# RWKV-5 attention into a multiplicative FFN: the FFN's first products start inside token chunk 0, on weight strips of 256 columns, and one predicated copy serves both heads of a pair

## The chip, the cores and the metric

The kernel runs on one core of one Trainium2 chip. The metric is the device time of one execution in microseconds (us); lower is better. The notes on the profile use its names for the engines: PE is TensorE (matrix products), PEld its weight loads, DVE is VectorE, ACT is ScalarE, POOL is GpSimd and SP is SyncE, which issues the transfers.

## The reference

```python
def attention(r, k, v, w, u):                 # (4, 8, 768, 48) = batch, heads, tokens, head size; float32
    state = zeros(B, H, D, D)
    for t in range(S):
        cur = einsum('bhd,bhe->bhde', u * k[:, :, t], v[:, :, t])
        y[:, :, t] = einsum('bhd,bhde->bhe', r[:, :, t], state + cur)
        state = w[:, :, None] * state + einsum('bhd,bhe->bhde', k[:, :, t], v[:, :, t])

x = y.transpose(0, 2, 1, 3).reshape(3072, 384)
out = (((x @ w1) * (x @ w2)) @ w3) @ w_out    # w1, w2: 384 x 1024; w3: 1024 x 1024; w_out: 1024 x 384
```

The four FFN weights come as float64; the attention's inputs are float32 and the result is float32.

## The kernel before

**Units.** The 768 tokens of each of the four sequences are cut into six chunks of 128. A unit is one chunk of one sequence, for all eight heads, and the units run chunk by chunk: unit n is chunk n // 4 of sequence n % 4. Heads are handled in four pairs, so that two heads of 48, padded to 64, fill 128 partitions.

**What a unit does.** `load` fetches k, r and v. `scale(n)` multiplies k and r by powers of the decay on VectorE (L277, tile `krs`), forms the sums for the diagonal on VectorE (L282 to L284, tiles `ruk` and `dg`) and writes them as diagonal matrices on ScalarE (L289, tile `AT`). `turn(n)` transposes k and r on TensorE and copies them out on ScalarE (`kT`, `rT`). `pairs(n)` computes the 128 x 128 products of keys and receptances of each head on TensorE (L307) and copies the causal half over the diagonal matrices with two predicated copies on VectorE (L310). `output(n)` adds the contribution of the state (L355, from chunk 1 on) and of the chunk itself (L363), and ScalarE copies the result, transposed, into `xT[c]`. `update(n)` computes k times v (L381) and adds it to the state `st` (L388, or L390 and L393).

**The FFN.** It works on whole token chunks of 4 x 128 = 512 tokens. `ab(c, j)` computes 128 of the 1024 hidden columns of x w1 (L403) and of x w2 (L408), ScalarE copies the first out (L405) and VectorE multiplies the two into a tile `abt` (L409). w3 and w_out are multiplied into one matrix `w34` once: `fold(j)` transposes 128 rows of w3 (L263) and multiplies them with w_out (L267). `o(c, b)` multiplies the `abt` tiles by `w34` (L414) and stores 128 rows of the result.

**The weights.** A float64 piece lands in one of three tiles `raw` as 64-bit words. `convert` rebuilds float32 from the two 32-bit halves in seven steps: |x| on ScalarE (L231), then on VectorE a product (L232), a mask with a shift (L234), a mask with an or (L235), a mask (L237), the low half scaled (L238) and the last add (L239). w1 and w2 are taken in twelve pieces of 128 rows by 512 columns: first the six that hold columns 0 to 511, then the other six.

**The order.** `beside[c]` is a list of FFN steps for each chunk. Beside each unit's steps (scale and turn of unit n+1; then pairs of n+1, output and update of n) an eighth of its chunk's list is put. In chunk 0 that is only the first six weight pieces; chunk 1 has the other six and `ab(0, j)` for all j; chunk 2 `ab(1, j)`, w_out and the folds 0 to 2; chunk 3 the other folds, `o(0, b)` and `ab(2, j)`:

```python
beside = [
    W12[0],
    merge(W12[1], AB(0, range(KH))) + AB(0, range(KH, KF)),
    merge(AB(1), WO + W3(range(3))),
    merge(AB(2, range(KH)), W3(range(3, KF))) + O(0) + AB(2, range(KH, KF)),
```

A planner then turns the written order into a queue for each engine, from its own costs and from what each instruction needs; each engine works through its queue in that order. The functions that the change touches:

Of the kernel before, what the change touches and what calls it, by code (L numbers as in the profile page):

```python
# [8 lines left out]
F32 = mybir.dt.float32  # L9
I32 = mybir.dt.int32  # L10
U32 = mybir.dt.uint32
U64 = mybir.dt.uint64
# [4 lines left out]
PSUM = bass.MemoryType.PSUM  # L17
# [3 lines left out]
def kernel(  # L21
# [27 lines left out]
    nc = tc.nc  # L49
    B, H, S, D = r.shape  # L50
    P = 128
    C = 128
# [3 lines left out]
    NP = H // 2  # L56
    DM = H * D
    DF = moe_w3.shape[0]
    KM = DM // P
    KF = DF // P  # L60
    NT = B * C
    LEVELS = 7
    PIECE = 512
    W_LOW, W_HIGH = 0.6, 1.6
    Q = 32
    PD = 2 * D
# [3 lines left out]
    def rows(i):  # L70
        return slice(i * PAD, (i + 1) * PAD)
# [11 lines left out]
    krin = [const.tile([C, 2, H, D], F32, name=f"krin{i}") for i in range(NIN)]  # L83
    vnat = [const.tile([C, H, PAD], F32, name=f"vnat{i}") for i in range(NV)]
    krs = [const.tile([C, 2, H, PAD], F32, name=f"krs{i}") for i in range(NS)]
    raws = [const.tile([P, PIECE], U64, name=f"raw{i}") for i in range(NRAW)]
    st = [const.tile([P, NP, PD], F32, name=f"st{b}") for b in range(B)]
    wucol = const.tile([P, NP, 1], F32)
    nc.vector.memset(wucol, 1.0)
# [10 lines left out]
    NU = len(units)  # L100

    def load(n):
        if n >= NU:
# [9 lines left out]
    w34 = const.tile([P, KF, DM], F32)  # L113


    ab_pieces = [(dst[:, q, js], src[q * P:(q + 1) * P, js])
                 for js in (slice(z * PIECE, (z + 1) * PIECE) for z in range(DF // PIECE))
                 for q in range(KM) for dst, src in ((w1, moe_w1), (w2, moe_w2))]
    sent = [0]

    def fetch(piece):

        dst, src = piece
        if src.dtype != U64:
            nc.sync.dma_start(out=dst, in_=src)
            return None
        raw = raws[sent[0] % NRAW][:, :src.shape[1]]
        sent[0] += 1
        nc.sync.dma_start(out=raw, in_=src)
        return raw  # L130
# [57 lines left out]
    def body(arm, fast):  # L188
        tab = arm.enter_context(tc.tile_pool(name="tab", bufs=1))
        work = arm.enter_context(tc.tile_pool(name="work", bufs=2))  # L190
        psT = arm.enter_context(tc.tile_pool(name="psT", bufs=2, space=PSUM))
        psA = arm.enter_context(tc.tile_pool(name="psA", bufs=2, space=PSUM))
        psM = arm.enter_context(tc.tile_pool(name="psM", bufs=2, space=PSUM))
        psF = arm.enter_context(tc.tile_pool(name="psF", bufs=2, space=PSUM))

# [26 lines left out]
        def convert(piece, raw):  # L222
            dst, src = piece
            if src.dtype != U64:
                return
            n = src.shape[1]
            lo, hi = (raw.bitcast(U32).rearrange("p (n z) -> p n z", z=2)[:, :, z] for z in range(2))
            t, power = (work.tile([P, PIECE], F32, tag="cv", bufs=4, name=nm)[:, :n] for nm in ("t", "power"))
            tb, hb, pb = t.bitcast(U32), dst.bitcast(U32), power.bitcast(U32)

            nc.scalar.activation(out=power, in_=hi.bitcast(F32), func=ABS)  # L231
            nc.vector.scalar_tensor_tensor(dst, power, 1.125 * 2.0 ** -15, hi.bitcast(F32), ALU.is_ge, ALU.mult)  # L232

            nc.vector.tensor_scalar(tb, hb, 0x07FFFFFF, 3, ALU.bitwise_and, ALU.logical_shift_left)  # L234
            nc.vector.scalar_tensor_tensor(hb, hb, 0xC0000000, tb, ALU.bitwise_and, ALU.bitwise_or)  # L235

            nc.vector.tensor_scalar(pb, hb, 0xFF800000, None, ALU.bitwise_and)  # L237
            nc.vector.scalar_tensor_tensor(t, lo, 2.0 ** -52, power, ALU.mult, ALU.mult)  # L238
            nc.vector.tensor_add(dst, dst, t)  # L239

        def weight(piece):
            convert(piece, fetch(piece))
# [3 lines left out]

        def out_weight(c):
            wo[c] = work.tile([P, DM], F32, tag="wo", bufs=KF, name=f"wo{c}")
            weight((wo[c], moe_w_out[c * P:(c + 1) * P, :]))

        def w3_weight(j, z):
            if z == 0:
                w3n[j] = work.tile([P, DF], F32, tag="w3", bufs=3, name=f"w3n{j}")
            js = slice(z * PIECE, (z + 1) * PIECE)
            weight((w3n[j][:, js], moe_w3[j * P:(j + 1) * P, js]))

        def fold(j):
            w3T = work.tile([P, KF, P], F32, tag="w3", bufs=3, name=f"w3T{j}")
# [14 lines left out]
        def scale(n):  # L273

            kr = krin[n % NIN]
            if fast:
                nc.vector.tensor_mul(krs[n % NS][:, :, :, :D], kr, pn[:, :, :, :D])  # L277
            else:
                nc.scalar.copy(out=krs[n % NS][:, :, :, :D], in_=kr)
            ruk = work.tile([C, H, D], F32, tag="ruk", bufs=2, name=f"ruk{n}")  # L280
            dg = work.tile([C, H], F32, tag="dg", bufs=2, name=f"dg{n}")
            nc.vector.tensor_mul(ruk, kr[:, 0], kr[:, 1])  # L282
            nc.vector.tensor_mul(ruk, ruk, ub)
            nc.vector.tensor_reduce(dg, ruk, AX.X, ALU.add)  # L284
            AT[n] = work.tile([C, 2, NP, C], F32, tag="AT", bufs=2, name=f"AT{n}")
            for p in range(NP):
                for i in range(2):
                    h = 2 * p + i
                    nc.scalar.activation(out=AT[n][:, i, p, :], in_=ident, func=COPY, scale=dg[:, h:h + 1])  # L289
# [10 lines left out]
        def pairs(n):  # L300

            if fast:

                ps = [psA.tile([C, NP, C], F32, tag="a", name=f"ps_a{n}_{i}") for i in range(2)]
                for p in range(NP):
                    for i in range(2):
                        nc.tensor.matmul(ps[i][:, p, :], lhsT=kT[n][rows(i), p, :], rhs=rT[n][rows(i), p, :],  # L307
                                         start=True, stop=True)
                for i in range(2):
                    nc.vector.copy_predicated(AT[n][:, i], later.bitcast(I32)[:, None, :].to_broadcast([C, NP, C]), ps[i])  # L310
                return
            for l in range(LEVELS):
                L = 1 << l
# [81 lines left out]

        abt = {}

        def ab(c, j):
            abt[c, j] = work.tile([P, NT], F32, tag="abt", bufs=2 * KF + KF // 2, name=f"abt{c}_{j}")
            js = slice(j * P, (j + 1) * P)  # L400
            pa = psF.tile([P, NT], F32, tag="f", name=f"ps_a{c}_{j}")
            for q in range(KM):
                nc.tensor.matmul(pa, lhsT=w1[:, q, js], rhs=xT[c][:, q, :], start=(q == 0), stop=(q == KM - 1))  # L403
            a = work.tile([P, NT], F32, tag="sa", bufs=2, name=f"a{c}_{j}")
            nc.scalar.copy(out=a, in_=pa)  # L405
            pb = psF.tile([P, NT], F32, tag="f", name=f"ps_b{c}_{j}")
            for q in range(KM):
                nc.tensor.matmul(pb, lhsT=w2[:, q, js], rhs=xT[c][:, q, :], start=(q == 0), stop=(q == KM - 1))  # L408
            nc.vector.tensor_mul(abt[c, j], pb, a)  # L409

        def o(c, b):
            po = psF.tile([P, DM], F32, tag="f", name=f"ps_o{c}_{b}")
# [6 lines left out]
            nc.sync.dma_start(out=out[row:row + C, :], in_=osb)  # L419


        def AB(c, js=range(KF)):
            return [lambda c=c, j=j: ab(c, j) for j in js]

        def O(c):
            return [lambda c=c, b=b: o(c, b) for b in range(B)]

        def first(i):
            if i not in landed:
                landed[i] = fetch(ab_pieces[i])  # L430
            convert(ab_pieces[i], landed[i])

        half = len(ab_pieces) // 2
        W12 = [[lambda i=i: first(i) for i in range(z * half, (z + 1) * half)] for z in range(2)]
        WO = [lambda c=c: out_weight(c) for c in range(KF)]

        def W3(js):
            return [s for j in js for s in ([lambda j=j, z=z: w3_weight(j, z) for z in range(DF // PIECE)]
                                            + [lambda j=j: fold(j)])]

        def merge(*lists):

            keyed = [((i + 0.5) / len(x), m, s) for m, x in enumerate(lists) for i, s in enumerate(x)]
            return [s for _, _, s in sorted(keyed, key=lambda e: e[:2])]

        KH = KF // 2
        beside = [
            W12[0],
            merge(W12[1], AB(0, range(KH))) + AB(0, range(KH, KF)),
            merge(AB(1), WO + W3(range(3))),  # L450
            merge(AB(2, range(KH)), W3(range(3, KF))) + O(0) + AB(2, range(KH, KF)),
            merge(O(1) + O(2), AB(3)),
            merge(O(3), AB(4)),
        ]
# [4 lines left out]
        turn(0)  # L459
        pairs(0)  # L460
        for c in range(NCH):
            done = 0
            for b in range(B):
                n = c * B + b
                load(n + 2)
                steps = []
                if n + 1 < NU:
                    steps += [lambda: (scale(n + 1), turn(n + 1))]
                steps += [lambda: (n + 1 < NU and pairs(n + 1), output(n), update(n))]
                for i, step in enumerate(steps):  # L470
                    step()
                    due = len(beside[c]) * (b * len(steps) + i + 1) // (B * len(steps))
                    while done < due:
                        beside[c][done]()
                        done += 1
        for step in tail:
            step()
        landed.clear()
# [38 lines left out]
```

## Time and profile before

| | |
|---|---|
| median of 3 runs | 564.75 us (563.84 to 565.81) |
| the profiled execution: its time | 564.53 us |
| its span in the profile | 562.7 us |
| PE busy, share of the span | 539.0 us, 96% |
| PE weight loads busy | 307.2 us, 55% |
| VectorE busy | 255.5 us, 45% |
| ScalarE busy | 169.2 us, 30% |
| TensorE's mean granted clock | 0.989 |
| DMA | 37.52 MB, mean 67 GB/s |

Shares are over the whole span, but the kernel has stages with different limits, so the slices in time say more than the means. A busy TensorE is not one at its peak: matmuls are pipelined, and one of 128x512 lasts 597 ns in the table while the next begins 430 ns after it. The matmul records count passes: an fp32 matmul shows as two.

### The profile page before, as it was taken

The numbers are of one execution on the slowest core, as the hardware profiler recorded it, in microseconds if no ns is written. First come the engines' busy times: TensorE is split into PE (matmuls) and PEld (weight loads), VectorE is DVE, ScalarE is ACT, GpSimd is POOL, SyncE is SP. The second block draws the span as 40 slices with busy tenths as digits, with TensorE's granted clock in tenths as the row PEclk, the third lists the DMA queues.
The fourth block names the chain that finished last, engine by engine and source line by source line (L and its number), as shares of the span: only waits on it lengthen the run. The fifth ranks groups of instructions, "written<-read, shape, count | busy, mean of one in ns | idle before, by whom it ended". The sixth has DMA issues, their size and how long they took to land.

```text
span 562.7 us, 8088 instructions
## 1 busy us (share of the span) xinstructions
PE 539.0 (96%) x3304; PEld 307.2 (55%) x3304; DVE 255.5 (45%) x495; ACT 169.2 (30%) x400; POOL 3.6 (1%) x17
## 2 busy tenths in 40 slices
PE   3869999999999999999999999999999999999996
PEld 2656555455655565565645556555555555544453
DVE  5999999998674696840220414233211100001100
ACT  3745544454433263331211213122132110111010
POOL 2000000000000000000000000000000000000000
PEclk9969999999999999999999999999999999999999
DMA  7956543554233243220110202021010000000001
GB/s 161 227 134 160 153 112 90 149 170 132 43 115 77 76 120 97 57 43 21 50 29 14 57 14 57 15 57 30 16 29 14 1 15 14 29 28 0 0 16 47
DMA packets 84129, 37.52 MB, mean 67 GB/s; under 512 B 76273, under 2 KB 79474, under 8 KB 84082
## 3 DMA queue, kind: packets, MB, share of 16 engines
q1 hardware_dynamic: 84082, 36.91, 25.0%
q8 instruction: 28, 0.46, 0.3%
q14 instruction: 19, 0.16, 0.1%
HBM read 32.18 MB, written 4.72 MB: 66 GB/s over the span
## 4 chain that ended last, share of the span: by engine, by line
PE 90%; DVE 6%; DMA 1%; issue 1%; ACT 1%; SPq 0%; DVEq 0%; ACTq 0%
PE ps_o L414 22%; PE ps_b L408 22%; PE ps_a L403 22%; PE ps_w L267 7%; PE ps_a L307 5%; PE ps_y L363 4%; PE ps_y L355 3%; PE ps_kT L295 2%; PE ps_s L381 2%; PE ps_rT L295 2%; PE ps_w3T L263 1%; DVE t L238 1%; DVE AT L310 1%; DMA raw<-in_moe_w_dram 1%; DVE w L239 1%
## 5 line engine op out<-in xcount | busy, mean ns | idle before, releaser
L403 PE MATMUL ps_a<-xT,w 128*128 128x512 f32 x288 | 133.4, 597 | 0.7 <-DVE w L239 0.7
L409 DVE TENSOR_TENSOR abt<-ps_b,a 128x512 f32<-128x512 f32 x48 | 33.1, 691 | 221.8 <-PE ps_b L408 196.5
L408 PE MATMUL ps_b<-xT,w 128*128 128x512 f32 x288 | 132.5, 594 | 0.1
L414 PE MATMUL ps_o<-w,abt 128*128 128x384 f32 x384 | 127.2, 488 | 0.0
L414 PEld LDWEIGHTS ps_o<-w,abt 128*128 128x128 f32 x384 | 72.0, 190 | 49.2 <-issue 2.0
L408 PEld LDWEIGHTS ps_b<-xT,w 128*128 128x128 f32 x288 | 54.2, 190 | 67.1 <-issue 63.5
L403 PEld LDWEIGHTS ps_a<-xT,w 128*128 128x128 f32 x288 | 52.9, 190 | 56.8 <-issue 50.1
L289 ACT ACTIVATE AT<-ident,dg 128x128 f32<-128x128 f32 x192 | 59.1, 391 | 1.7 <-DVE dg L284 1.7
L405 ACT COPY a<-ps_a 128x512 f32<-128x512 f32 x48 | 28.0, 584 | 104.3 <-PE ps_a L403 104.3
L310 DVE COPY_PREDICATED AT<-later,ps_a 128x512 f32<-128x512 int32 x48 | 33.0, 730 | 31.2 <-PE ps_a L307 30.9
L417 ACT COPY osb<-ps_o 128x384 f32<-128x384 f32 x24 | 11.5, 479 | 108.7 <-PE ps_o L414 85.7
L267 PE MATMUL ps_w<-wo,w3T 128*128 128x384 f32 x128 | 43.1, 490 | 0.0
L307 PEld LDWEIGHTS ps_a<-rT,kT 64*128 64x128 f32 x384 | 25.9, 198 | 19.2 <-issue 11.3
L307 PE MATMUL ps_a<-rT,kT 64*128 64x128 f32 x384 | 31.7, 299 | 2.7 <-ACT rT L298 2.7
L367 ACT COPY xT<-ps_y 128x384 f32<-128x384 f32 x24 | 11.5, 478 | 74.3 <-PE ps_y L363 74.3
L231 ACT ACTIVATE power<-raw 128x512 f32<-128x512 f32 (+1 forms) x36 | 23.6, 655 | 31.5 <-DVE t L238 19.7
L267 PEld LDWEIGHTS ps_w<-wo,w3T 128*128 128x128 f32 x128 | 23.7, 190 | 15.7 <-ACT w3T L264 0.6
L363 PE MATMUL ps_y<-AT,vnat 128*32 128x128 f32 x768 | 29.1, 274 | 2.4 <-DVE AT L310 1.3
L298 ACT COPY kT<-ps_kT 128x512 f32<-128x512 f32 x24 | 14.0, 585 | 40.7 <-PE ps_kT L295 40.7
L363 PEld LDWEIGHTS ps_y<-AT,vnat 128*32 128x32 f32 x768 | 22.4, 110 | 5.2 <-DVE AT L310 2.5
L277 DVE TENSOR_TENSOR krs<-krin,pn_in 128x768 f32<-128x768 f32 x24 | 22.9, 956 | 3.8 <-ACT pn_in L179 2.8
L238 DVE SCALAR_TENSOR_TENSOR t<-raw,power 128x512 f32<-128x512 uint32 (+1 forms) x36 | 23.6, 655 | 0.2
(64 smaller groups left out, 339.1 us busy)
## 6 DMA issues: line engine op xcount, KB each, us to landing
raw<-in_moe_w_dram SPq DMA_DIRECT2D x28, 512.0 KB, 3.6
krin<-in_k_dram SPq DMA_DIRECT2D x24, 192.0 KB, 2.8
krin<-in_r_dram SPq DMA_DIRECT2D x24, 192.0 KB, 3.4
vnat<-in_v_dram SPq DMA_DIRECT2D x24, 192.0 KB, 2.8
out_dram<-osb SPq DMA_DIRECT2D x24, 192.0 KB, 1.9
raw<-in_moe_w_out_dram SPq DMA_DIRECT2D x8, 384.0 KB, 2.9
ub<-in_u_dram SPq DMA_DIRECT2D x1, 192.0 KB, 5.3
wucol<-in_w_dram SPq DMA_DIRECT2D x2, 0.8 KB, 1.9
```

What stands on the lines that cost most here:

```text
L231: nc.scalar.activation(out=power, in_=hi.bitcast(F32), func=ABS)
L238: nc.vector.scalar_tensor_tensor(t, lo, 2.0 ** -52, power, ALU.mult, ALU.mult)
L267: nc.tensor.matmul(ps, lhsT=w3T[:, kc, :], rhs=wo[kc], start=(kc == 0), stop=(kc == KF - 1))
L289: nc.scalar.activation(out=AT[n][:, i, p, :], in_=ident, func=COPY, scale=dg[:, h:h + 1])
L307: nc.tensor.matmul(ps[i][:, p, :], lhsT=kT[n][rows(i), p, :], rhs=rT[n][rows(i), p, :], start=True, stop=True)
L310: nc.vector.copy_predicated(AT[n][:, i], later.bitcast(I32)[:, None, :].to_broadcast([C, NP, C]), ps[i])
L363: nc.tensor.matmul(to(q, g), lhsT=vv[:, p, x:x + Q], rhs=AT[n][:, i, p, :], start=(not c and m < P // Q), stop=True, skip_group_check=True)
L403: nc.tensor.matmul(pa, lhsT=w1[:, q, js], rhs=xT[c][:, q, :], start=(q == 0), stop=(q == KM - 1))
L405: nc.scalar.copy(out=a, in_=pa)
L408: nc.tensor.matmul(pb, lhsT=w2[:, q, js], rhs=xT[c][:, q, :], start=(q == 0), stop=(q == KM - 1))
L409: nc.vector.tensor_mul(abt[c, j], pb, a)
L414: nc.tensor.matmul(po, lhsT=abt[c, j][:, b * C:(b + 1) * C], rhs=w34[:, j, :], start=(j == 0), stop=(j == KF - 1))
```

## The change

The weights w1 and w2 come in eight strips of 256 columns by all 384 rows (three groups of 128), w1 and w2 in turn, instead of twelve pieces of 128 rows by 512 columns. The tiles `raw` and the scratch of `convert` grow from 512 to 768 elements a partition, and the scratch has three buffers instead of four.

In chunk 0, after unit 1's output, `ab(0, 0)` and `ab(0, 1)` are computed for the first 256 tokens, that is the two sequences that are ready; for the other 256 at the end of the chunk, and behind them `ab(0, 2)` and `ab(0, 3)`. Chunk 1 keeps `ab(0, 4)` to `ab(0, 7)`. The lists of chunks 0 and 1 say for each of eight places what stands there; the lists of later chunks are cut in eighths as before.

`pairs` writes the products of both heads of the pairs into one PSUM tile of two banks, in one buffer, and one predicated copy of 1024 elements a partition takes the place of two of 512.

`abt` has 18 buffers instead of 20 and `ruk` one instead of two, and in chunk 3 two of `ab(2, j)` instead of four are merged with the folds.

```diff
+    STRIP = 256
+    RAW = KM * STRIP
...
-    ab_pieces = [(dst[:, q, js], src[q * P:(q + 1) * P, js])
-                 for js in (slice(z * PIECE, (z + 1) * PIECE) for z in range(DF // PIECE))
-                 for q in range(KM) for dst, src in ((w1, moe_w1), (w2, moe_w2))]
+    ab_pieces = [(dst[:, :, js], src.rearrange("(q p) n -> p q n", p=P)[:, :, js])
+                 for js in (slice(z * STRIP, (z + 1) * STRIP) for z in range(DF // STRIP))
+                 for dst, src in ((w1, moe_w1), (w2, moe_w2))]
...
-        psA = arm.enter_context(tc.tile_pool(name="psA", bufs=2, space=PSUM))
+        psA = arm.enter_context(tc.tile_pool(name="psA", bufs=1 if fast else 2, space=PSUM))
...
-            n = src.shape[1]
-            lo, hi = (raw.bitcast(U32).rearrange("p (n z) -> p n z", z=2)[:, :, z] for z in range(2))
-            t, power = (work.tile([P, PIECE], F32, tag="cv", bufs=4, name=nm)[:, :n] for nm in ("t", "power"))
+            _, m, n = src.shape
+            lo, hi = (raw.bitcast(U32).rearrange("p m (n z) -> p m n z", z=2)[:, :, :, z] for z in range(2))
+            t, power = (work.tile([P, RAW], F32, tag="cv", bufs=3, name=nm)[:, :m * n].rearrange("p (m n) -> p m n", m=m)
+                        for nm in ("t", "power"))
...
-                ps = [psA.tile([C, NP, C], F32, tag="a", name=f"ps_a{n}_{i}") for i in range(2)]
+                ps = psA.tile([C, 2, NP, C], F32, tag="a", name=f"ps_a{n}")
...
-                for i in range(2):
-                    nc.vector.copy_predicated(AT[n][:, i], later.bitcast(I32)[:, None, :].to_broadcast([C, NP, C]), ps[i])
+                nc.vector.copy_predicated(AT[n].rearrange("s i p t -> s (i p) t"),
+                                          later.bitcast(I32)[:, None, :].to_broadcast([C, H, C]),
+                                          ps.rearrange("s i p t -> s (i p) t"))
...
-        def ab(c, j):
-            abt[c, j] = work.tile([P, NT], F32, tag="abt", bufs=2 * KF + KF // 2, name=f"abt{c}_{j}")
+        def ab(c, j, ts=slice(0, NT)):
+            if (c, j) not in abt:
+                abt[c, j] = work.tile([P, NT], F32, tag="abt", bufs=2 * KF + 2, name=f"abt{c}_{j}")
...
-                nc.tensor.matmul(pa, lhsT=w1[:, q, js], rhs=xT[c][:, q, :], start=(q == 0), stop=(q == KM - 1))
+                nc.tensor.matmul(pa[:, :n], lhsT=w1[:, q, js], rhs=xT[c][:, q, ts], start=(q == 0), stop=(q == KM - 1))
...
-            nc.vector.tensor_mul(abt[c, j], pb, a)
+            nc.vector.tensor_mul(abt[c, j][:, ts], pb[:, :n], a[:, :n])
...
-        half = len(ab_pieces) // 2
-        W12 = [[lambda i=i: first(i) for i in range(z * half, (z + 1) * half)] for z in range(2)]
+        W12 = [[lambda i=i: first(i) for i in (2 * z, 2 * z + 1)] for z in range(DF // STRIP)]
...
+        halves = [slice(0, NT // 2), slice(NT // 2, NT)]
+        none = []
         beside = [
-            W12[0],
-            merge(W12[1], AB(0, range(KH))) + AB(0, range(KH, KF)),
+            [none, none, none, W12[0] + AB(0, range(0, 2), halves[0]), none, W12[1][:1], none,
+             AB(0, range(0, 2), halves[1]) + W12[1][1:] + AB(0, range(2, 4))],
+            [none, W12[2], none, AB(0, range(4, 6)), none, W12[3], none, AB(0, range(6, 8))],
             merge(AB(1), WO + W3(range(3))),
-            merge(AB(2, range(KH)), W3(range(3, KF))) + O(0) + AB(2, range(KH, KF)),
+            merge(AB(2, range(2)), W3(range(3, KF))) + O(0) + AB(2, range(2, KF)),
```

## The prediction

> **What bounds the kernel now.** I read the slices of the span first, then stage windows, then the order of time at the last place where TensorE waits, then the groups of VectorE with their shapes kept apart.
>
> ```profile
> PE   3869999999999999999999999999999999999996
> DVE  5999999998674696840220414233211100001100
> PEclk9969999999999999999999999999999999999999
> ...
> 28.00:42.00 14.00, 8.85 (x90) 7.17 (x90) 13.19 (x26) 6.96 (x18) 0.00 (x0) 0.63 0.54 136
> 42.00:56.00 14.00, 13.61 (x189) 8.53 (x191) 13.55 (x27) 7.90 (x22) 0.00 (x0) 1.00 0.66 159
> 84.00:98.00 14.00, 13.32 (x99) 7.10 (x94) 13.66 (x28) 6.07 (x15) 0.00 (x0) 1.00 0.31 85
> 98.00:112.00 14.00, 14.00 (x63) 7.00 (x55) 13.91 (x33) 6.79 (x16) 0.00 (x0) 1.00 0.58 155
> 112.00:126.00 14.00, 14.00 (x120) 7.96 (x119) 13.96 (x31) 6.75 (x17) 0.00 (x0) 1.00 0.56 154
> ```
>
> After a window's length come the busy times of PE, weight loads, VectorE, ScalarE, GpSimd, the granted clock, DMA share and GB/s. VectorE is busy from 14 to 126 us almost without a hole; TensorE has holes only early. The last that matters is this one:
>
> ```profile
> 84.13 0.68 DVE L239 TENSOR_TENSOR w<-w,t 128x512 f32<-128x512 f32 x1
> ...
> 84.86 1.13 PE L403 MATMUL ps_a<-xT,w 128*128 128x512 f32 x2 [0.68 <-DVE w L239]
> ...
> 109.27 0.60 PE L295 MATMUL ps_kT<-ident,krs 128*128 128x128 f32 x4
> ```
>
> At 84.86 the matmul that had waited for the last add (L239) of a w1 piece starts. From there TensorE runs on without a hole that counts (one of 0.24 us near 206) until its last matmul near 558; the chain of waits gives it 90% of the span. At 109.27 the last `ab` of token chunk 0, `ab(0, 7)`, is through and unit 8's transposes begin. Behind this point both kernels have the same matmuls. **So the change is worth the shift of this landmark, and what TensorE waits afterwards.** What sets it is VectorE: six of the seven steps by which a weight piece is rebuilt from float64 stand on it, between the attention's own steps.
>
> ```profile
> L310 DVE COPY_PREDICATED AT<-later,ps_a 128x512 f32<-128x512 int32 x8 | 5.8, 726 | 0.1
> L235 DVE SCALAR_TENSOR_TENSOR w<-w,t 128x512 uint32<-128x512 uint32 x8 | 5.5, 686 | 0.1
> ...
> L277 DVE TENSOR_TENSOR krs<-krin,pn_in 128x768 f32<-128x768 f32 x4 | 3.8, 950 | 0.0
> L234 DVE TENSOR_SCALAR t<-w 128x512 uint32<-128x512 uint32 x8 | 3.3, 416 | 0.0
> L237 DVE TENSOR_SCALAR power<-w 128x512 uint32<-128x512 uint32 x8 | 3.3, 414 | 0.0
> ```
>
> The two mask steps L234 and L237 take 415 ns where L235 takes 686 for as many elements[...]. Durations overlap, so I count from start to start: 0.60 us for a two-source step of 512, 0.47 for one of 384, 0.87 for one of 768 (L277, 62.12 to 62.99); a mask step 0.335 for 512, 0.27 for 384; a predicated copy 0.62.
>
> [...] In the trace both are one run of 512, and the steps are fast; no run shows another shape yet. [...] at 20.63 VectorE waits 0.42 us for the state update's matmuls (L381) and the next weight step comes after. [...] The trace has 0.50 from 31.5 to 38.5 after a window with 1.85 of 3.5 us busy[...].
>
> **The change, part by part.** The VectorE orders of the two built programs can be laid side by side. In the new one, the scaling of unit 8's keys stands behind all eight strips and eight predicated copies. TensorE behind it: turn, ScalarE's copy of rT, pairs, update of unit 7, two of three matmuls of `ps_a`, then `ps_b`, `ps_a`, `ps_b`, which end at the landmark. From turn to pairs 1.8 us (76.36 to 78.18), pairs 1.1 (115.38 to 116.48), the rest of y and the update 0.7, four passes of 0.43 and three times 2.58 (from the starts between 98.86 and 109.27) 9.45, the handoff 0.1: 13.15 us.
>
> *Strips.* Twelve pieces of 512 columns become eight of 3 x 256 = 768 elements. A piece cost 4 x 0.60 + 2 x 0.335 = 3.07, twelve 36.8 us. A strip costs 4 x 0.87 plus two mask steps. Those now read `w1[:, :, js]`, three rows of 256 that do not touch, and write a tile that is one run of 768: outermost 3 against 768, [...] 0.87 as for L277; [...] they would be 0.47 (0.067 per 128 elements from 384 to 512, on top of 0.335). No row of before shows it: between 0.47 and 0.87 I take 0.87, **16 x 0.40 = 6.4 us** apart[...]. Eight strips: 8 x 5.22 = 41.8 us, 5.0 more than before; at the fast rate 35.4.
>
> *One predicated copy.* 1024 elements for twice 512: 0.62 + 0.53 (four times the 0.13 from 384 to 512 elements) = 1.15 against 1.24, so 0.09 a unit, 0.7 us over the eight at the landmark; bounds 0 and 0.7[...]. The single PSUM buffer of two banks holds what two of one bank held: the next unit's pairs wait for this unit's copy in both.
>
> *Halves.* `ab(0, 0)` and `ab(0, 1)` become four of 256 tokens: 24 matmul passes of about 0.215 for 12 of 0.43, nothing on TensorE as weight loads (0.19) still fit under them; two more ScalarE copies, beside other work; two more VectorE products, 4 x 0.335 for 2 x 0.60, 0.14 us.
>
> *Sum on VectorE* from its start at 10.65 to unit 8's scaling: 9 scalings 7.8, 32 steps of 384 for ruk and dg 15.0, 8 copies 9.2, 7 state updates 5.3 and two decays 0.9, strips 41.8, six products 3.7, three steps of the first w_out piece 1.2: 84.9, so 95.5. To this come waits. The same sum for before ends at 80.95 where the trace has 84.81: 3.9 us, of which 2.7 are named waits. For after: the two first strips are 768 KB instead of 512 and stand in the queue before units 1 and 2's loads, so unit 1's scaling starts 262 KB/(227 GB/s of the page's second slice) = 1.2 us later, 1.8 in all; 0.3 where the last update matmul of unit 1 is queued behind unit 2's turn; 1.1 of small gaps as before; 0.4 for half-clock matmuls between 35 and 42. I take 3.6, bounds 2 and 6. Later queue steps cost nothing here: raw tile 4 is asked for near 33 and used at 52, tile 6 near 52 and 66. Landmark: 95.5 + 3.6 + 13.15 = **112.25, 3.0 us later than 109.27**.
>
> *Fewer buffers for abt (18), conversion scratch (3) and ruk (1).* The plan for chunk 3 now puts fold 3 right behind fold 2 and fold 5 right behind fold 4, with no `ab` between. Each waits for a tile's last conversion: behind the product after `ps_b`, VectorE needs about 8.7 us, TensorE arrives after 8.3. About 0.3 us each, 0.24 already there before: 0.4 more, bounds 0 and 6.2 (one full tile, 3.1 us, at each). The scratch's third buffer lets the next |x| be taken during a conversion, as the order shows.
>
> Sum: +3.0 + 0.4 = +3.4 us against the profiled execution, which took 564.53 us (span 562.7 and 1.8 around it), 567.9 us; the median of the runs, 564.75, lies 0.2 above that execution, less than the rounding here.
>
> **The rivals.** *Faster[...].* [...] Price: 16 x 0.40 = 6.4 us less, so 95.5 becomes 89.1, the landmark 105.8, and the end 564.5 - 3.5 + 0.4 = 561.4. It decides below 0.66 us a mask step, where 16 x 0.21 eats up the loss. *No difference:* a slower VectorE is waited for less often, TensorE's work is always ready, the half-clock stretch costs nothing, and waits shrink from 3.6 to 1.5: landmark 110.1, fold waits as before, 565.3. *Slower still:* folds 3 and 5 each wait most of a tile: +3.0 + 4 = 571.5. For it, VectorE's order there has four tiles in a row with three raw buffers; against, the fold near 206 waited 0.24 only. That the early `ab` does not happen is excluded: in the built order the first half matmuls stand before unit 2's pairs.
>
> **How the numbers follow.** About 0.3%, 1.7 us, is what a measurement of this kernel tells from no change. Slow masks, as worked out: 0.60, from 565.9 to 570; slower still 0.08; no difference 0.14; fast masks 0.18. The range 562.3 to 571.0 leaves out a good part of the fast case (0.12) and the worst (0.07). Faster 0.18, same 0.14, slower 0.68; the likeliest value is 567.9.
>
> **What would show it.** Groups of VectorE by shape: mask steps of 768 near 0.95 us in duration (right) or near 0.55 (wrong, and then the kernel is faster). Predicated copies of 1024 near 1.26 us. Unit 8's first transpose at about 112; TensorE without holes from there but for the folds. VectorE without long waits between 45 and 100. If the landmark lies at 112 and the end is still not later, the folds or the tail are misread; if mask steps are slow and the landmark is early, the share of VectorE in the bound is.

## The result and the profile after

| | before | after |
|---|---|---|
| median | 564.99 us (563.84 to 565.81, 4 runs) | 570.76 us (570.39 to 571.22, 4 runs) |
| the profiled execution, its span | 564.53 us, 562.7 us | 571.22 us, 569.1 us |

The ratio is 1.0104 [1.0084, 1.0124]: the changed kernel is slower by 5.8 us. The forecast was 567.9 us with a range from 562.3 to 571.0. The direction was right and the median lies just inside the range, but the loss is nearly twice as large as forecast (5.8 us, where the forecast is 3.2 above the median of before that it started from).

The busy slices of the changed kernel and its granted clock come first, then the order of time on TensorE in the last stretch before the landmark of the prediction. One name in the prediction was wrong: the transposes at the landmark are those of unit 9 (they are the tenth group of `ps_kT`, and the count of units begins at 0). The scaling of unit 8 and `ab(0, 7)`, to which its sums are counted, are named rightly.

```profile
PE   2778989999999999999999999999999999999997
...
DVE  4999999999685879740040314042211100001100
...
PEclk9899989899999999999999999999999999999999
```

```profile
99.82 0.96 DVE L281 TENSOR_TENSOR krs<-krin,pn_in 128x768 f32<-128x768 f32 x1
...
100.83 0.66 PE L299 MATMUL ps_kT<-ident,krs 128*128 128x128 f32 x4 [1.65 <-DVE krs L281]
101.32 0.97 PE L299 MATMUL ps_rT<-ident,krs 128*128 128x128 f32 x4
102.22 1.51 PE L368 MATMUL ps_y<-AT,vnat 128*32 128x128 f32 x24
103.66 1.69 PE L311 MATMUL ps_a<-rT,kT 64*128 64x128 f32 x16
...
115.78 0.60 PE L299 MATMUL ps_kT<-ident,krs 128*128 128x128 f32 x4
```

Unit 8's scaling begins at 99.82 us and lets the next step start at 100.69, not at 99.1 as forecast. TensorE has then waited 1.65 us for it. From there to unit 9's first transpose it takes 15.1 us where 13.15 were forecast. The landmark lies at 115.78: 6.5 us later than before, and 3.5 later than forecast. Behind it nothing is lost: from landmark to the end of the span it is 453.4 us before (562.7 - 109.27) and 453.3 after (569.1 - 115.78). The window over the last stretch shows the clock (columns as in the prediction, the clock third from the end):

```profile
101.00:104.00 3.00, 3.00 (x34) 2.22 (x35) 2.97 (x8) 1.73 (x3) 0.00 (x0) 0.57 0.78 143
104.00:106.00 2.00, 2.00 (x32) 1.68 (x32) 1.28 (x3) 0.23 (x1) 0.00 (x0) 0.80 0.49 183
```

The groups of VectorE by shape, over the stretch in which the weights are rebuilt, answer to the prediction's first test. Mean durations are in ns:

```profile
L313 DVE COPY_PREDICATED AT<-later,ps_a 128x1024 f32<-128x1024 int32 x9 | 11.7, 1299 | 0.8 <-PE ps_a L311 0.7
L239 DVE SCALAR_TENSOR_TENSOR w<-w,t 128x768 uint32<-128x768 uint32 x8 | 7.6, 951 | 0.0
L238 DVE TENSOR_SCALAR t<-w 128x768 uint32<-128x768 uint32 x8 | 7.6, 946 | 0.0
L241 DVE TENSOR_SCALAR power<-w 128x768 uint32<-128x768 uint32 x8 | 7.6, 944 | 0.0
```

The mask steps L238 and L241 take as long as the two-source step L239 beside them (946 and 944 ns against 951): the faster rate that they had before (416 and 414 against 686, at 512 elements) is gone. And the waits of VectorE up to 105 us, in total, number and longest:

```profile
DVE krs L281 <- ACT pn_in L182: 2.8, 1, 2.8
DVE krs L281 <- DMA krin<-in_r_dram: 2.2, 1, 2.2
DVE st L395 <- PE ps_s L386: 1.2, 1, 1.2
DVE st L393 <- PE ps_s L386: 0.9, 2, 0.7
```

The first of them lies ahead of the start of the prediction's sum. The second is unit 1's load, which is queued between the two first strips; the last two are state updates that come late from TensorE. The longest of these, 1.2 us at 81.02, comes right behind a stretch at a granted clock of 0.50 (77.51 to 80.92).

### The profile page after: what moved, and what is told of

Its sections match the earlier page's. It is cut to its first block, busy times and chain, and to the rows that moved or that the text cites. A ratio compares the mean times of both kernels' runs of the same rounds, so it can differ in the third digit from the quotient of the medians.

```text
span 569.1 us, 8064 instructions
## 1 busy us (share of the span) xinstructions
PE 538.9 (95%) x3328; PEld 312.0 (55%) x3328; DVE 263.2 (46%) x449; ACT 169.5 (30%) x398; POOL 3.6 (1%) x17
## 4 chain that ended last, share of the span: by engine, by line
PE 80%; DVE 14%; issue 2%; DMA 2%; SPq 1%; ACT 0%; DVEq 0%; ACTq 0%
PE ps_o L421 22%; PE ps_a L410 19%; PE ps_b L415 19%; PE ps_w L271 6%; PE ps_y L368 3%; PE ps_a L311 3%; PE ps_y L360 2%; DMA krin<-in_r_dram 2%; PE ps_s L386 2%; DVE t L238 1%; PE ps_kT L299 1%; PE ps_rT L299 1%; DVE power L241 1%; DVE t L242 1%; DVE w L243 1%
## 5 line engine op out<-in xcount | busy, mean ns | idle before, releaser
L416 DVE TENSOR_TENSOR abt<-ps_b,a 128x512 f32<-128x512 f32 (+1 forms) x50 | 33.4, 668 | 231.6 <-PE ps_b L415 206.6
L410 PE MATMUL ps_a<-xT,w 128*128 128x512 f32 (+1 forms) x300 | 133.8, 580 | 0.0
L415 PE MATMUL ps_b<-xT,w 128*128 128x512 f32 (+1 forms) x300 | 132.1, 576 | 0.7 <-DVE abt L416 0.6
L415 PEld LDWEIGHTS ps_b<-xT,w 128*128 128x128 f32 x300 | 56.6, 190 | 68.0 <-issue 63.4
L410 PEld LDWEIGHTS ps_a<-xT,w 128*128 128x128 f32 x300 | 55.4, 190 | 55.3 <-issue 49.7
L412 ACT COPY a<-ps_a 128x512 f32<-128x512 f32 (+1 forms) x50 | 28.3, 567 | 106.6 <-PE ps_a L410 106.5
L313 DVE COPY_PREDICATED AT<-later,ps_a 128x1024 f32<-128x1024 int32 x24 | 31.6, 1315 | 15.5 <-PE ps_a L311 15.4
L235 ACT ACTIVATE power<-raw 128x512 f32<-128x512 f32 (+2 forms) x32 | 22.9, 714 | 44.6 <-DVE w3n L243 20.6
L299 PE MATMUL ps_kT<-ident,krs 128*128 128x128 f32 x96 | 15.8, 291 | 8.8 <-DVE krs L281 7.5
```

The source lines that it names most:

```text
L299: nc.tensor.transpose(ps[:, p, :], krs[n % NS][:, g, 2 * p:2 * p + 2, :].rearrange("t h d -> t (h d)"), ident)
L313: nc.vector.copy_predicated(AT[n].rearrange("s i p t -> s (i p) t"), later.bitcast(I32)[:, None, :].to_broadcast([C, H, C]), ps.rearrange( ...
L410: nc.tensor.matmul(pa[:, :n], lhsT=w1[:, q, js], rhs=xT[c][:, q, ts], start=(q == 0), stop=(q == KM - 1))
L412: nc.scalar.copy(out=a[:, :n], in_=pa[:, :n])
L415: nc.tensor.matmul(pb[:, :n], lhsT=w2[:, q, js], rhs=xT[c][:, q, ts], start=(q == 0), stop=(q == KM - 1))
L416: nc.vector.tensor_mul(abt[c, j][:, ts], pb[:, :n], a[:, :n])
```

## The experiments

Two theories stood at the start. **Masks:** the slow mask steps on VectorE are the loss. **More than masks:** the late load, TensorE's half clock or the early halves carry a part of it that the prediction had too small. Runs of one batch shared a chip and the kernel before; its median there was 564.2 to 564.7 us. Ratios are against it.

### The mask steps

Three versions of the changed kernel alter only the shapes that the two mask steps see. TensorE's order up to the landmark and VectorE's order up to unit 8's scaling are the same in all three traces as in the changed kernel's.

flat: the strips are stored one after another, so that a mask step sees one run of 768.

```diff
-    w1 = const.tile([P, KM, DF], F32)
+    w1 = const.tile([P, DF // STRIP, KM, STRIP], F32)
...
-    ab_pieces = [(dst[:, :, js], src.rearrange("(q p) n -> p q n", p=P)[:, :, js])
+    ab_pieces = [(dst[:, z], src.rearrange("(q p) n -> p q n", p=P)[:, :, z * STRIP:(z + 1) * STRIP])
```

> The changed kernel with w1 and w2 kept strip by strip (three rows of 256 of a strip lie behind each other), so that both mask steps read and write one run of 768 elements; transfers, plan and matmuls as in the changed kernel. Theory A[...]: mask steps of 768 fall from 0.95 to about 0.55 us, VectorE has 16 x 0.40 = 6.4 us less before unit 8's scaling, unit 8's first transpose comes at about 109.5 instead of 115.8, the time is 6.3 us less: about 564.5 us. Rival B (TensorE's half-clock stretches and the waits that follow each other set the landmark, and a faster VectorE only waits longer): 2 us less or not at all, 568.5 to 571 us.

pad: the weights stay, and the scratch gets three rows with gaps.

```diff
-            t, power = (work.tile([P, RAW], F32, tag="cv", bufs=3, name=nm)[:, :m * n].rearrange("p (m n) -> p m n", m=m)
+            t, power = (work.tile([P, KM * (STRIP + 2)], F32, tag="cv", bufs=3, name=nm)[:, :m * (n + 2 * (m > 1))].rearrange("p (m n) -> p m n", m=m)[:, :, :n]
```

> The changed kernel with the two scratch tiles t and power as three rows of 256 with a gap of two elements between them, so that source and destination of a mask step both have three rows (odd and equal) instead of three rows against one run of 768; the weights stay as they are. [...] a mask step has a mean of 0.55 us as with flat weights, and the time is that run's, 562 to 563. Rival[...]: mask steps stay at 0.945 us and the time at 570.8.

evenview: weights and scratch stay, and the mask steps see both as two halves.

```diff
+            two = (lambda x: x.rearrange("p m (z n) -> p z m n", z=2)) if m > 1 else (lambda x: x)
-            nc.vector.tensor_scalar(tb, hb, 0x07FFFFFF, 3, ALU.bitwise_and, ALU.logical_shift_left)
+            nc.vector.tensor_scalar(two(tb), two(hb), 0x07FFFFFF, 3, ALU.bitwise_and, ALU.logical_shift_left)
```

> The changed kernel, its weights stored as before; only the two mask steps of a strip see source and destination as two halves of three rows of 128 columns instead of three rows of 256: outermost 2 on both sides. Theory[...]: mask steps near 0.55 us mean, as with one run, and the end at 562 to 563. Rows cost something as in the run with padded scratch, where three rows took 0.683 (0.13 more than one run): 0.68 to 0.82 us and 564.5 to 567. Rival, the strided source alone decides: 0.945 us and 570.8.

The same two groups of VectorE in flat, then in pad, then in evenview:

```profile
L238 DVE TENSOR_SCALAR t<-w 128x768 uint32<-128x768 uint32 x8 | 4.4, 553 | 0.0
L241 DVE TENSOR_SCALAR power<-w 128x768 uint32<-128x768 uint32 x8 | 4.4, 550 | 0.0
```

```profile
L238 DVE TENSOR_SCALAR t<-w 128x768 uint32<-128x768 uint32 x8 | 5.5, 683 | 0.0
L241 DVE TENSOR_SCALAR power<-w 128x768 uint32<-128x768 uint32 x8 | 5.4, 681 | 0.0
```

```profile
L239 DVE TENSOR_SCALAR t<-w 128x768 uint32<-128x768 uint32 x8 | 4.4, 552 | 0.0
L242 DVE TENSOR_SCALAR power<-w 128x768 uint32<-128x768 uint32 x8 | 4.4, 549 | 0.0
```

| version | mask step, mean | start to start | time | ratio to before |
|---|---|---|---|---|
| flat | 0.55 us | 0.47 us | 562.25 us | 0.9957 [0.9941, 0.9972] |
| evenview | 0.55 | 0.47 | 562.84 | 0.9969 [0.9957, 0.9980] |
| pad | 0.68 | 0.60 | 564.67 | 1.0007 [0.9995, 1.0018] |
| changed kernel | 0.945 | 0.86 | 570.76 | 1.0104 [1.0084, 1.0124] |

The mask steps alone decide the sign. Between evenview and the changed kernel nothing differs but how the two steps see their operands; with two halves the rows are shorter and more, yet the steps are as fast as over one run (0.552 us against 0.553). For three rows on both sides my expectation of 0.55 us fell: pad has 0.683, which is 0.131 above the two halves and 0.262 below the 0.945 of three rows against one run. Why it lies there is not shown by these runs.

Unit 8's scaling and the landmark in flat:

```profile
92.33 0.96 DVE L281 TENSOR_TENSOR krs<-krin,pn_in 128x768 f32<-128x768 f32 x1
...
106.80 0.60 PE L299 MATMUL ps_kT<-ident,krs 128*128 128x128 f32 x4
```

In time the dose is not one for one. From the changed kernel to flat VectorE loses 16 x 0.39 = 6.3 us of work and the time 8.5. Flat's landmark is at 106.80, 9.0 earlier: 6.3 of it are masks, 1.45 fewer waits of VectorE (2.8 us instead of 4.25), 1.5 a shorter last stretch (13.60 instead of 15.09), less 0.3 of other steps.

slowmask goes the other way: the kernel before, the two mask steps of its twelve pieces written as two-source steps (the second of them is shown).

```diff
-            nc.vector.tensor_scalar(pb, hb, 0xFF800000, None, ALU.bitwise_and)
+            nc.vector.scalar_tensor_tensor(pb, hb, 0xFF800000, hb, ALU.bitwise_and, ALU.bitwise_and)
```

> The kernel before, with nothing changed but the two mask steps of the twelve w1 and w2 pieces, written as two-source steps with the same result[...]: 0.60 instead of 0.335 us each, 24 x 0.265 = 6.4 us more on VectorE, the same dose as in the changed kernel. Theory A (VectorE's sum sets the landmark one for one): 564.9 + 6.0 = about 571 us, as slow as the changed kernel, although the rest of the change is not there. Rival B (the masks' share is small): under 2 us more, at most 567 us.

Measured: 567.49 us, 1.0064 [1.0042, 1.0086]. The steps take 0.68 us instead of 0.415, 24 x 0.265 = 6.4 us more on VectorE, of which 3.2 us reach the time and 1.75 the landmark of the profiled execution (111.02). So in the order of before VectorE does not set the landmark alone: theory A fell, and the prediction's reading of the kernel before was too simple there. There TensorE has work almost all the time from 42 to 82 us (busy 39.52 of 40), which is the likely reason that about half is hidden; how much a longer stretch at half clock (0.50, 13.65 us from 31.04 on, where the kernel before has 10.24) adds was not separated. The changed order hides nothing of it.

### The clock in the last stretch

In flat the rows behind unit 8's turn take 0.60 (ps_rT), 0.86 (y) and 1.16 us (pairs) at a clock of 1.00, in the changed kernel, at 0.57 from 101 to 104 us, 0.97, 1.51 and 1.69, in the same order of TensorE. To make this a test, fillers were put where TensorE waits.

warm has eight filler transposes ahead of each of the first nine units' turns; gate8 has 24 ahead of unit 8's turn alone:

```diff
+                for p in range(24 if fast and g == 0 and n == 8 else 0):
+                    nc.tensor.transpose(ps[:, p % NP, :], ident, ident)
```

> The changed kernel with eight filler transposes (about 0.9 us of TensorE work, overwritten afterwards) ahead of the transposes of each of the first nine units, where TensorE waits 1.2 to 1.8 us for the scaling. It keeps the array busy. Theory A2 (the half-clock stretches at 22 to 26, 77 to 81 and 101 to 104 us, after such waits, are the part of the miss that I had priced at 0.4): granted clock 1.0 in all of these, unit 8's first transpose about 2 to 3 us earlier, 568 to 569 us. Rival (the clock costs nothing, since VectorE is what is waited for): no change or up to 3 us more from fillers that TensorE executes late, 571 to 574 us.

> The changed kernel with 24 filler transposes of the identity ahead of one turn only, that of unit 8, in the 1.65 us in which TensorE waits for this unit's scaling. The instruction order of VectorE up to unit 8's scaling stays that of the changed kernel. Theory half clock (the missing 1.5 us of the last stretch are the transposes, y and pairs at a clock of 0.57 after a poorly filled TensorE): the stretch from unit 8's scaling to unit 9's first transpose falls from 15.1 to about 13.6 us (the 13.60 of the run with flat weights), the clock between 101 and 104 is 1.00, and the end comes 1 to 1.5 us earlier: 569.3 to 569.8. Rival, the order and not the clock: the stretch stays at 15 and the time at 570.8.

Measured: 571.36 us, 1.0124 [1.0105, 1.0142], and 571.84 us, 1.0144 [1.0124, 1.0165]. Neither gained, though the clock was 1.00 behind unit 8's scaling in both. The planner had moved other work for the fillers. In warm seven more w_out steps (3.3 us of busy time) stand on VectorE ahead of unit 8's scaling; VectorE waits only 1.1 us instead of 4.25, and the scaling begins at 100.00 all the same. In gate8 a w1 matmul step of `ab(0, 6)` and the rest of unit 7's y fall behind the turn, and the stretch is 15.9 us. Both runs are inconclusive on the clock.

gate8b takes eight fillers of one column. The order of TensorE then differs by one matmul of y.

```diff
+                for p in range(8 if fast and g == 0 and n == 8 else 0):
+                    nc.tensor.matmul(ps[:, 0, :1], lhsT=ident, rhs=ident[:, :1], start=True, stop=True)
```

> The changed kernel with 8 filler matmuls of one column ahead of unit 8's turn, short enough that the order of TensorE stays, but for one matmul of y (0.03 us), what the changed kernel has. Theory half clock: with the clock at 1.00 between 101 and 105 the stretch from unit 8's scaling to unit 9's first transpose falls from 15.1 to 13.6 us, and the end comes 1 to 1.5 us earlier, 569.3 to 569.8. If fillers of one column do not hold the clock, stretch and time stay at 15.1 and 570.8, and nothing is decided.

The order of time on TensorE in gate8b:

```profile
95.40 1.95 PE L299 MATMUL ps_kT<-ident 128*128 128x1 f32 x16
...
99.72 0.66 PE L301 MATMUL ps_kT<-ident,krs 128*128 128x128 f32 x4 [0.41 <-DVE krs L281]
100.21 0.60 PE L301 MATMUL ps_rT<-ident,krs 128*128 128x128 f32 x4
100.74 1.06 PE L370 MATMUL ps_y<-AT,vnat 128*32 128x128 f32 x26
101.73 1.16 PE L313 MATMUL ps_a<-rT,kT 64*128 64x128 f32 x16
...
113.31 0.60 PE L301 MATMUL ps_kT<-ident,krs 128*128 128x128 f32 x4
```

The pairs are back at 1.16 us. From the end of unit 8's scaling (98.70 + 0.87) to unit 9's first transpose it is 13.74 us instead of 15.09: the half clock costs 1.35 us here. flat, pad and evenview, which have no fillers and the order of the changed kernel, took 13.6 at full clock (1.00; flat and pad 13.60). The other 1.1 us by which gate8b's landmark is earlier (113.31) lie ahead of the scaling, where VectorE waited less for the load: 0.9 us instead of 2.2. The time was 569.96 us, 1.0107 [1.0089, 1.0126], in another batch than the changed kernel's. So both were run once more side by side.

> The changed kernel itself, on one chip with the three others, as what they are compared with: 570.8 within 0.5, with the half clock (0.57 and 0.50) at 101 to 105 us and a stretch of 15 us from unit 8's scaling to unit 9's first transpose.

> The version with 8 one-column fillers ahead of unit 8's turn once more, beside the changed kernel on one chip. Theory half clock: 1 to 1.5 us below it, as the stretch of 13.74 instead of 15.09 says. Rival, what the stretch wins comes back elsewhere: no difference.

again, the changed kernel: 570.90 us (570.45 to 572.87, 4 runs), 1.0113 [1.0092, 1.0133], its stretch 15.10 us. gate8c, a copy of gate8b: 569.12 us (568.98 to 571.39, 6 runs), 1.0097 [1.0077, 1.0117], its stretch again 13.74 us. The medians differ by 1.8 us in the expected direction, but the intervals overlap: the 1.35 us are shown in the trace, and in the time only indicated. The half clock does not come at a fixed place: in the first profile of the changed kernel its 0.50 begins at 22.90, 77.51 and 101.40 us, in again's at 37.58, 78.54 and 102.43. But each of these stretches lasts 3.41 us, and within a profile their beginnings are whole multiples of 3.41 apart (16 and 7 in the first, 12 and 7 in the second).

The start has no record of the clock: the first one of the changed kernel begins at 19.48 us, and where there is none the windows read 1.00. The rows ahead of it take the durations of half clock: 1.09 us for ps_kT at 11.74, where 0.66 is taken at 28.51, and 2.08 for the pairs at 16.34, where those at 81.95 take 1.16.

What TensorE's rows fill of the stretches of 3.41 us, called windows here, suggests what decides. In the changed kernel, from 19.48 to 111.6 us, the three windows ahead of the half clock are filled to 17, 43 and 41%, every other to 55% or more. pad waited 1.50 us for the same scaling and kept its clock there (1.00): its window, 92.78 to 96.19, is filled to 56%. So in these traces a wait well under one window, 1.65 us of 3.41, came ahead of half clock where it left the window less than about half full. The limit is not sharp: the kernel before lost the clock behind a window of 53% (from 28.05), and loads kept it behind one of 52% (from 74.50).

gateall adds fillers ahead of the pairs of units 1 and 3 and of the turn of unit 6, in the same manner.

> The changed kernel with one-column fillers where its trace has TensorE idle ahead of a half-clock stretch: 12 ahead of the pairs of units 1 and 3, 8 ahead of the turns of units 6 and 8; the order of TensorE is kept but for four matmuls of y. Theory half clock: the clock is 1.00 up to 110 us, VectorE's waits for slowed matmuls (0.7 for the pairs, 0.9 and 1.2 for the state updates) shrink by 2 us and the last stretch is 13.7: 567.5 to 568.5, the forecast. Rival, VectorE's sum and the wait for unit 1's loads: no more than gate8c, 569.3 to 570.8.

Measured: 571.50 us, 1.0141 [1.0118, 1.0164], with single runs from 568.40 to 573.71. The profiled execution is the fastest of them. In it the clock between 76 and 80 us is 1.00, VectorE's wait of 1.2 us for a state update is gone, unit 8's scaling begins at 97.26 and the landmark is at 113.00. But the clock is now low from 96.87 to 100.28 us (0.72 in the mean of 98 to 102), and the other executions are later, so the run decides nothing about the time. It does bear on the fillers, for this stretch comes right behind the same sixteen passes that stand in gate8b, and y at its start takes 1.50 us where gate8b has 0.86:

```profile
93.96 1.95 PE L299 MATMUL ps_kT<-ident 128*128 128x1 f32 x16
...
96.80 1.50 PE L366 MATMUL ps_y<-rT,st 128*32 128x128 f32 x24
```

The window ahead of it, 93.45 to 96.87, is full with the fillers and 49% full without them. The same holds for the window from 18.36, 97% with and 24% without, behind which the clock fell as well; behind two others, full with them and 48 and 49% without, it stayed. In gate8b the window from 96.04 is filled to 61% even without its fillers. So it is not shown that fillers of one column hold the clock; gate8b had a full clock, and that is all its comparison needs. With gate8's 24 whole transposes the window from 96.56 is 56% full, without them 7%, and the clock stayed at 1.00.

evenfill shows one way in which such fillers cost. It is evenview with the twelve fillers ahead of the pairs of units 1 and 3.

```diff
+                if n in (1, 3):
+                    fill = psT.tile([P, NP, C], F32, tag="t", name=f"ps_fill{n}")
+                    for p in range(12):
+                        nc.tensor.matmul(fill[:, 0, :1], lhsT=ident, rhs=ident[:, :1], start=True, stop=True)
```

> The version with two halves of three rows in the mask steps and 12 one-column fillers ahead of the pairs of units 1 and 3, with the order of both engines kept. Its runs without fillers lie at 559.9 to 561.7 where the mean clock was 0.997 or more and mostly at 562.6 to 564.1 where it was less. Theory half clock: all runs at 560 to 561.5. Rival, fillers delay the pairs: 562.8 or later.

Measured: 564.26 us, 0.9992 [0.9979, 1.0004]. The records of the clock in the profiled execution have 1.00 throughout, and the kernel is still slower than evenview, by 0.23% or 1.3 us by the ratios (the two intervals just touch). The pairs stand behind the fillers and VectorE waits for them, as its order of time shows:

```profile
25.55 1.31 DVE L318 COPY_PREDICATED AT<-later,ps_a 128x1024 f32<-128x1024 int32 x1 [2.50 <-PE ps_a L316]
```

The rival holds: the fillers cost VectorE 2.5 us there. They stand ahead of these records, where TensorE is still slow: the 24 passes at 18.28 take 5.12 us and those at 35.51 take 2.74, the pairs at 23.33 take 2.08 and those at 33.93 take 1.16. That they bought the clock is not shown, since the records of evenview's own profile have 1.00 throughout without them. Of evenfill's 22 runs the eight with a mean clock of 1.000 took 564.05 to 565.39 us, while the four fastest (561.59 to 562.22) had 0.997.

### Load, early halves, predicated copy

loads sends unit 1's transfers ahead of both strips instead of between them.

```diff
-    landed = {0: fetch(ab_pieces[0])}
     load(1)
+    landed = {0: fetch(ab_pieces[0])}
     landed[1] = fetch(ab_pieces[1])
```

> The changed kernel with unit 1's r, k and v sent ahead of both first strips instead of between them. Theory queue (unit 1's scaling starts 2.16 us late because 1.5 MB of strips share the 16 DMA engines with it): the wait for krin falls from 2.2 to 0.6 us or less, the first conversion starts up to 2 us later but VectorE has unit 1's steps meanwhile, and what is won is at most 1.6 us: 569.2 to 570.8. Rival: the wait varied between 0.6 and 2.2 in runs with this same order, so it isn't the order of the queue, and later waits take up what it frees: 570.8. Second rival: the first strip comes late instead and VectorE waits for that, 571.5.

Measured: 571.62 us, 1.0142 [1.0116, 1.0167]. The wait for k and r is gone, but VectorE now waits 2.1 us for the first strip's |x|, and 1.7 us for two of the early products. The second rival holds: whichever comes second is waited for. With the strips ahead of the load, as in the changed kernel, the wait for unit 1's k and r came out between 0.5 and 2.2 us from run to run.

noearly leaves out the early halves: `ab(0, 0)` and `ab(0, 1)` run whole at the end of chunk 0. flatnoearly does the same to flat.

```diff
-            [none, none, none, W12[0] + AB(0, range(0, 2), halves[0]), none, W12[1][:1], none,
-             AB(0, range(0, 2), halves[1]) + W12[1][1:] + AB(0, range(2, 4))],
+            [none, none, none, W12[0], none, W12[1][:1], none,
+             AB(0, range(0, 2)) + W12[1][1:] + AB(0, range(2, 4))],
```

> The changed kernel without the early start: ab(0, 0) and ab(0, 1) are computed for all 512 tokens at the end of chunk 0, not half after unit 1; strips, buffers and the single predicated copy stay. Theory A (VectorE sets the landmark, so matmuls moved forward gain nothing): within 1 us of the changed kernel, 570 to 571.5 us, perhaps 0.3 less for two products fewer. Rival C (the early matmuls do fill TensorE, 5.2 us of them): 573 us or more.

> The strips stored one after another (mask steps at 0.55 us) and without the early halves: ab(0, 0) and ab(0, 1) whole at the end of chunk 0. Asks what the early start of the second part is worth once the masks are fast. Theory VectorE (the landmark follows VectorE's work and the stretch behind unit 8's scaling, where no matmul of the early halves stands): 562.0 to 563.0, as with them. Rival, early work fills TensorE's holes and saves it: without it 1.7 us or more later (four matmul passes of 0.43 a unit of ab), 564 to 566.

Measured: noearly 571.07 us, 1.0117 [1.0098, 1.0135], no different from the changed kernel; flatnoearly 564.71 us, 1.0000 [0.9988, 1.0013], 0.43% or 2.4 us above flat by the ratios. So the early start shows nothing in the time while VectorE is slow, and about 2.4 us with fast masks. The first of these is in part luck of the clock: in noearly too unit 8's scaling comes 0.9 us later than in the changed kernel (100.73), behind six more w_out steps, but its last stretch kept the clock (1.00 from 98 to 118 us; 13.74 us instead of 15.09), and its landmark is at 115.34. My theory for flatnoearly fell. Its landmark is 1.7 us later than flat's (108.53), and so is unit 8's scaling (93.92 instead of 92.33): the planner has put six more w_out steps ahead of it, about 2.4 us of VectorE. Whether the early halves help by themselves or by keeping these steps back was not separated.

onecopy is the kernel before with the merged predicated copy and its PSUM tile alone.

```diff
-                ps = [psA.tile([C, NP, C], F32, tag="a", name=f"ps_a{n}_{i}") for i in range(2)]
+                ps = psA.tile([C, 2, NP, C], F32, tag="a", name=f"ps_a{n}")
```

> The kernel before with one part of the change alone: one predicated copy of 1024 for both heads of a pair, and the one PSUM tile of two banks that goes with it. Theory: a copy of 1024 takes 1.20 from start to start where two of 512 take 1.24, so eight give 0.3 us at most and the time stays at 563.9 to 564.2. Rival: pairs of the next unit wait for the copy of both halves, and y waits for the whole copy where its first half sufficed: 565 to 566.

Measured: 563.24 us, 0.9984 [0.9973, 0.9994]. The part helps by about 1 us, more than the 0.3 us of its copies; the rival's waits did not come. In its profile the landmark is at 107.10, 2.2 us earlier, and VectorE has none of the four waits, 2.6 us in all, that the kernel before has between 10.65 and 85 us (1.1 for loads, 1.5 for TensorE). Whether they went with the part or differ from execution to execution stays open.

## Why the prediction was right and where it was wrong

**The bound and the landmark: right.** All of the loss lies ahead of the landmark, and the stretch behind it has the same length within 0.1 us. In it the folds waited 1.02 us instead of 0.24 (forecast 0.4 more), but this does not show at its end.

**The mask steps: right.** They take 0.86 us from start to start against 0.87, which was the author's assumption for a shape that no run of before had (0.47 is the estimate at the rate of before), and flat gives 6.3 us for sixteen against 6.4. flat and evenview confirm the rival with fast masks as well: 561.4 forecast, 562.25 and 562.84 measured.

**The predicated copy and the halves: nearly right.** 1.20 us instead of 1.15, so 0.04 and not 0.09 a unit is saved; the products of 256 take 0.335 as forecast.

**VectorE's sum: right.** From 10.63 up to and with unit 8's scaling the steps take 84.94 + 0.87 = 85.8 us, small gaps between them included. The prediction had 84.9 and 1.1 for small gaps, 86.0.

**VectorE's waits: the first term that was mis-sized.** The prediction had 2.5 us of named waits: 1.8 for the load, 0.3 for a state update, 0.4 for matmuls at half clock. The trace has 4.25: 2.16 for the load and 0.72, 0.17 and 1.20 for state updates. The last goes with the half clock: it comes right behind the 0.50 of 77.51 to 80.92, in which the update's products take 1.10 us. It is there again in the profiles of again, gate8 and gate8c, where unit 6's ps_kT takes 0.86 to 1.12 us at that place (0.87 in the changed kernel), and gone in those of gateall and loads, where it takes 0.66, and in gate8b's. Whether the 0.72 is one too is not separated: evenview still waits 0.54 there, but its pairs just ahead, at 20.73, take 2.08 us as well. This term is the scaling's 1.6 us (4.25 - 2.5, less the 0.2 that the sum had too much).

**The last stretch on TensorE: the step that failed.** 13.15 us were forecast, 15.09 measured. The prediction took every duration in it at full clock, though it had just read a granted clock of 0.50 in the kernel before, from 31.5 to 38.5 us, behind a window with 1.85 of 3.5 us busy. gate8b took 13.74 at full clock: 1.35 us were half clock. Most of the remaining 0.6 us are addends: in flat, at full clock, the stretch took 13.60, with 0.14 for the start of the turn, which was left out, and y and update 0.95 instead of 0.7.

**From landmark to time.** 115.78 - 112.25 = 3.5 us of miss at the landmark are 1.6 and 1.9. The medians miss by less, 570.76 - 567.9 = 2.9: the profiled execution of after is 0.46 us above its median, and the 0.4 us that the prediction added for the folds did not reach the end, while 0.3 more than before lie outside the span. Of the rivals, slower still (571.5) comes near in its number, but not by its mechanism, the folds.

**Why TensorE waited longer than the prediction saw:** flat, evenview and the changed kernel have the same order of TensorE, which suggests that the planner's costs do not know the lost rate. Then the queue is laid for the fast masks, and TensorE comes to unit 8's turn 1.65 us early instead of 1.05 (flat) and waits there in line, with `ab` behind it. That was there to be read: the built order was compared, but only VectorE's times were laid over it.

## What to carry to other kernels

When a tile becomes part of a larger one, look at what the fast steps see: a single-source step over three rows against one run took 0.945 us instead of 0.55, and two halves on both sides brought the rate back without moving any data. Where one engine's lateness makes TensorE wait more, price the half clock behind the wait: a stretch of 3.41 us at a granted clock of 0.50 does 1.7 us of work less, by estimate (half of 3.41), and 1.35 were measured here. A filler or an earlier load changes a planned order, so compare the orders of all engines before reading its time, and ask of a filler whether the clock would have been full without it.

flat and evenview are faster than both kernels, by 2.0 and 1.4 us against before on their chips.

## What the runs showed of the hardware that was not expected

A mask step over three rows on both sides ran at neither rate: 0.683 us for 768 elements, between 0.552 and 0.945. In the changed kernel TensorE's clock fell to 0.50 for windows of 3.41 us behind windows that were 17, 43 and 41% full, in pad not behind one of 56%; in gateall sixteen passes of one column that filled such a window from 49 to 100% did not prevent it. And executions of one kernel differ: evenview's eighteen runs go from 559.93 to 564.13 us, its three whose records have a mean clock of 1.000 from 559.93 to 561.44. That the clock makes this difference is not shown; evenfill speaks against it.
